# One load for the value rows of a block's neighbouring chunks, memory rows copied by GpSimd, and a planner that counts eight transfers: a fused attention and two-layer MoE kernel on one core

## The chip, the core and the metric

The kernel runs on one core of a Trainium2 chip. The metric is the device time of the whole program in microseconds (us). The core has TensorE for matrix products, VectorE, ScalarE and GpSimd for elementwise work, SyncE (SP) for issuing transfers, and 16 DMA engines that serve all queues. The profile calls the first four PE, DVE, ACT and POOL, PE's weight loads PEld, and SP's queue of transfers SPq.

## The reference: what is computed

```python
# attention, per batch and head: chunks of 32 queries, 16 keys to the left, 8 to the right, 8 memory keys
for c in range(nc):                       # B, H, S, D = 4, 8, 768, 64
    k_full = concat(mem_k, k[c*32-16 : c*32+40]);  v_full = concat(mem_v, v[same rows])
    scores = (q_c @ k_full.T) / sqrt(D)
    a = exp(scores - max); a = a / (sum(a) + 1e-9)
    out[c] = a @ v_full
x = out as 3072 tokens x 512
h = x @ w_in;  g = h * clip(h + 3, 0, 6) / 6;  x = g @ w_out          # layer 0, d_ff = 2048
h = x @ w_in2; g = where(h >= 1, h, where(h <= -1, 0, (h + 1)**2 / 4)); out = g @ w_out2   # layer 1
```

## The kernel before, in words

The 3072 tokens are worked in six tiles of 512 (`T`), and a tile is four attention blocks of 128 queries, that is four chunks of 32 (`NSB`). There are 24 blocks, numbered 0 to 23 here. The inputs lie in memory by groups of 96 queries (`QB`, index j). A group has a row block of queries and keys, and 120 rows of values: 8 memory rows, 16 to the left, 96, 8 to the right. For the first `NEARLY` groups queries, keys and values lie in one array `qkv` with value rows of 2 KB; for the later groups they lie in `qk` and `vv`, and a value row there comes in two pieces of 1 KB.

A block takes these steps. `load_block` brings queries and keys of a group (tile `q_sb`, 448 KB). `load_values` brings the values of the block's four chunks (tile `v_sb`, 512 KB: for each chunk 8 memory rows and 56 others). `scores` (L460) multiplies on PE into PSUM tiles `sc`; DVE and ACT make the softmax; DVE turns it (tile `tr`); `values` multiplies it on PE with `v_sb` into `pv` (L529 in blocks 0 to 7, L519 later); ACT and DVE write the result as a high and a low part (`xhi`, `xlo`). When four blocks are done, their tile goes through `hidden` (PE writes `ph`, L603 to L605: three products for each piece, high times high, high times low, low times high) and `project` (PE writes `py` in layer 0 and `po` in layer 1). The weights come packed (`raw`, 512 KB each, 64 of them) and are unpacked by ACT and DVE (L286 to L312) into `w`, two for each f of 16 in a layer.

The order of all work is made by a planner, `Plan`, before the program runs. Each task has a key (when it is due), the engines it can run on with an assumed duration, and the tiles it reads and writes; `run` steps through time and gives each engine its next task. The order on each engine is thus fixed at build time, and on the chip each engine takes its instructions in that order and waits where a tile is not ready. SP's order is the order in which it can issue loads. A load can't be issued before its tile's slot is free: the pool `in` has two slots (queries and keys), `lv` two (values), `o` two (outputs), `w` 33 (raw and unpacked weights, and for the first four blocks also loads and softmax tiles).

Up to a planned time of 60 us (`FILL`) the program puts unused products of a tile of zeros, here called fillers (L765), into gaps that the plan foresees on PE:

```python
while at + ns <= t.start + more:
    P.matmul(c, warm, warm[:, :n].unsqueeze(1).to_broadcast([128, m, n]), start=True, stop=True, ...)
    at += ns
```

Their number is part of the program and doesn't depend on what happens on the chip. In the trace each float32 product of `scores` and `values` (L460, L519, L529) is two matmuls, each with a weight load of its own, so `x128` in the trace is `x64` in a list of the program's order. All other products are one.

Of the kernel before, what the change touches and what calls it, by code (L numbers as in the profile page):

```python
# [10 lines left out]
F32 = mybir.dt.float32  # L11
# [22 lines left out]
GRP = 4  # L34
NEARLY = 6
LATE_W = GRP * (QB + KB)
# [36 lines left out]
WINDOW = 100  # L73
CHANGE = 100


class Plan:
# [58 lines left out]
    def run(self, at):  # L136
        free = dict(at)
        bw = 0
        last_kind = None
        ready = {e: [] for e in free}  # L140
# [10 lines left out]
        while left:  # L151
            best = None
            for e, ts in ready.items():
                found = []
                blocked = set()
                for t in sorted(ts, key=lambda t: (t.key, t.n)) if e == "SP" else ts:
                    est = max(free[e], t.ready)
                    taken = [] if blocked & {p for b in t.bufs if not b.slot for p in b.pools} else self.slots_for(t)
                    if taken is None or len(taken) < sum(b.slot is None for b in t.bufs):
                        if e == "SP":  # L160

                            blocked.update(p for b in t.bufs if b.slot is None for p in b.pools)
# [12 lines left out]
                if best is None or est < best[0]:  # L175
                    best = est, e, t
# [50 lines left out]
def fused_kernel(ctx: ExitStack, tc: tile.TileContext, qkv, qk, vv, wpk, const, out):  # L227
# [40 lines left out]
    def weight(l, f, z, key, after=()):  # L268
# [45 lines left out]
        lo, hi = (raw, "lo"), (raw, "hi")  # L314
        add(("SP", 430), key - 4, load, writes=[lo, hi], kb=512, after=after)
        add([("DVE", dve(512, True)), ("ACT", 575)], key - 0.5, shift, writes=[lo])
# [14 lines left out]

    q_buf, v_buf = {}, {}
    WQ = NP * (QB + KB)
# [9 lines left out]
    def load_block(j, key):  # L343
# [17 lines left out]
        if not wide(j):  # L361
            add(("SP", 430), key - 6 - far, lambda e: nc.sync.dma_start(tile_of(q), src), writes=[(q, 0)], kb=448, after=after, line="load")
            return
        k4 = lambda: tile_of(q)[:, NP * QB:].rearrange("p (a t) -> p a t", a=NP)
        add(
            ("SP", 430), key - 6 - far, lambda e: nc.sync.dma_start(
                k4()[:, :, :KB], src[:, NP * QB:].rearrange("p (a t) -> p a t", a=NP)
            ), writes=[(q, 1)], kb=256, after=after, line="load",
        )
        add(  # L370
            ("SP", 430), key - 6 - far, lambda e: nc.sync.dma_start(tile_of(q)[:, :NP * QB], src[:, :NP * QB]),
            writes=[(q, 0)], kb=192, after=after, line="load",
# [12 lines left out]
    def load_values(s, key):  # L385
# [5 lines left out]
            ["lv"] + ["w"] * early, [128, 2, H * D], F32, "v_sb", **({"w": 1} if early else {}),  # L391
        )
        runs = []
        for c in range(NSB):
            j, i = divmod(s * NSB + c, NCH)
            cuts = [0] + [NMEM] * (i > 0) + [CHUNK] * (not late) + [KC]
            for a, b in zip(cuts, cuts[1:]):
                row = a if b <= NMEM else a + CHUNK * i
                p, col = (64 * (c % 2) + a, c // 2) if late else (CHUNK * c + a % CHUNK, a // CHUNK)
                for r in runs:  # L400
# [5 lines left out]
        for n, (j, row, p, col, m) in enumerate(sorted(runs, key=lambda r: (r[3], r[2]))):  # L406
            if j < NEARLY:
                src, rows = qkv[j, row:row + m, WQ:], lambda t: t
            else:
                g = 2 * (j - NEARLY)  # L410
                src, rows = vv[g:g + 2, row:row + m, :].rearrange("g k c -> k g c"), lambda t: t.rearrange("k (g c) -> k g c", g=2)
            add(
                ("SP", 430), key - 5 - 3 * (not early),
                lambda e, src=src, rows=rows, p=p, m=m, col=col: nc.sync.dma_start(rows(tile_of(v)[p:p + m, col]), src),
                writes=[(v, n)], kb=2 * m, line="load v",
            )
        v.parts = len(runs)

    def block(s, key):
# [90 lines left out]
        def values(e, m=None):  # L510
# [25 lines left out]
        add(  # L536
            ("PE", 750 if all(wide(j) for j in qs) else 1450), key - 4, scores,
            [(q_buf[j], x) for j in qs for x in range(1 + wide(j))],
# [10 lines left out]
        add(("DVE", dve(512)), key - 2.4, norm, [(sm, 3)], [(st, 0), (st, 1)])  # L549
        of_v = [(v, n) for n in range(v.parts)]  # L550
        if late:
            for c in chunks:
                for b in range(2):
                    add(("DVE", dve(256)), key - 2.2, lambda e, c=c, b=b: turn_part(e, c, b), [(st, 0), (st, 1)], [(tr, c, b)])
            ts = [(tr, c, b) for c in chunks for b in range(2)]
            add(("PE", 750), key - 1, values, [*ts, *of_v], [(x, 0) for x in pv], line="values", kind="a")
        else:
# [130 lines left out]
    def second_x(n):  # L688
        xhi, xlo = xbuf[NT + n]
        key = NK + NF * n  # L690
        for c in range(NC):
            x = Buf(["in", "o", "st"], [128, T], F32, "x2raw")
            add(
                ("SP", 430), key - 8 + 0.5 * c, lambda e, c=c, x=x: nc.sync.dma_start(tile_of(x), ymid[n, :, c]),
                [("ymid", n, c)], [(x, 0)], kb=256, after=[h_tasks[key - NF]],
# [140 lines left out]
```

## Time and profile before

| | |
|---|---|
| time before, median of 3 runs | 1162.21 us (1161.91 to 1163.37) |
| time of the profiled execution | 1161.94 us |
| its span in the trace | 1160.1 us |
| PE busy in the span | 1144.1 us, 99% |
| DVE, ACT, POOL busy | 614.9, 457.8, 0.2 us |
| first product of `hidden` starts | 54.42 us |

The trace counts from the start of the span; 1.8 us of the execution's time lie outside it. PE is busy nearly throughout, but the fillers count as busy too, so the busy share says little of the first 55 us.

### The profile page before, as it was taken

The page shows a single profiled execution, that of the slowest core. Times are in us where ns is not written, and L with a number is a line of the kernel's source. Part 1 is how long each engine was busy: PE and PEld are TensorE (multiplying, and loading weights), DVE is VectorE, ACT ScalarE, POOL GpSimd, SP SyncE. Part 2 cuts the span into 40 slices and gives each one's busy share as a digit, 9 for nine tenths or more (in the row PEclk, how much of TensorE's full clock was granted, in tenths as well). Part 3 has the DMA queues.
Part 4 walks back from the last instruction along what each step waited for, and adds up shares of the span by engine and source line. Part 5 has one row for each costly group of instructions (what it writes and reads, how often), then busy time and mean ns, then how long its engine had stood idle before and what let it go on. Part 6 is the DMA issues. An engine that isn't in the chain of part 4 may idle for free.

```text
span 1160.1 us, 20860 instructions
## 1 busy us (share of the span) xinstructions
PE 1144.1 (99%) x8766; PEld 939.5 (81%) x8766; DVE 614.9 (53%) x1116; ACT 457.8 (39%) x1083; POOL 0.2 (0%) x4
## 2 busy tenths in 40 slices
PE   8899999999999999999999999999999999999998
PEld 6687888888887888888888888888888888888887
DVE  2589955445555445643899634434434434433433
ACT  3599633334333333333788423223223223222221
POOL 0000000000000000000000000000000000000000
PEclk8699999999999999999999999999999999999999
DMA  6791131112112112210656300200200200000100
GB/s 207 249 396 55 57 100 35 51 54 90 48 35 87 51 51 74 70 38 19 200 183 216 91 1 1 73 1 1 73 1 1 73 1 1 37 1 1 37 1 37
DMA packets 48644, 81.05 MB, mean 70 GB/s; under 512 B 5158, under 2 KB 28582, under 8 KB 48550
## 3 DMA queue, kind: packets, MB, share of 16 engines
q1 hardware_dynamic: 48550, 79.71, 20.9%
q8 instruction: 69, 1.13, 0.4%
q14 instruction: 25, 0.20, 0.1%
HBM read 67.11 MB, written 12.58 MB: 69 GB/s over the span
## 4 chain that ended last, share of the span: by engine, by line
PE 97%; DMA 1%; issue 1%; ACT 1%; DVE 0%; SPq 0%; DVEq 0%; ACTq 0%
PE ph L603 15%; PE ph L604 15%; PE ph L605 15%; PE py L652 8%; PE po L657 8%; PE po L659 8%; PE po L658 8%; PE py L653 7%; PE py L654 7%; PE sc L460 2%; PE pv L529 2%; PE pv L519 1%; PE pv L765 1%; DMA ymid<-ysb 0%; DMA v_sb<-qkv 0%
## 5 line engine op out<-in xcount | busy, mean ns | idle before, releaser
L603 PE MATMUL ph<-xhi,w 128*128 128x512 f32 x768 | 300.5, 391 | 0.0
L604 PE MATMUL ph<-xlo,w 128*128 128x512 f32 x768 | 299.2, 390 | 0.0
L605 PE MATMUL ph<-xhi,w 128*128 128x512 f32 x768 | 299.0, 389 | 0.0
L626 ACT ACTIVATE r<-r,bias 128x512 f32<-128x512 f32 x96 | 69.3, 722 | 286.6 <-DVE r L623 286.6
L633 DVE TENSOR_TENSOR glo<-r,ghi 128x512 fp32r<-128x512 f32 x192 | 132.6, 690 | 81.9 <-ACT ghi L632 80.4
L632 ACT CAST ghi<-r 128x512 fp32r<-128x512 f32 x192 | 119.5, 623 | 133.7 <-DVE r L629 71.2
L603 PEld LDWEIGHTS ph<-xhi,w 128*128 128x128 f32 x768 | 144.5, 188 | 30.5 <-ACT raw L286 0.3
L605 PEld LDWEIGHTS ph<-xhi,w 128*128 128x128 f32 x768 | 144.3, 188 | 30.2
L604 PEld LDWEIGHTS ph<-xlo,w 128*128 128x128 f32 x768 | 144.5, 188 | 29.7
L652 PE MATMUL py<-ghi,w 128*128 128x512 f32 x384 | 153.5, 400 | 1.3 <-DVE ysb L679 1.3
L654 PE MATMUL py<-ghi,w 128*128 128x512 f32 x384 | 149.8, 390 | 0.0
L653 PE MATMUL py<-glo,w 128*128 128x512 f32 x384 | 149.8, 390 | 0.0
L657 PE MATMUL po<-w,ghi 128*128 128x512 f32 x384 | 149.4, 389 | 0.0
L658 PE MATMUL po<-w,ghi 128*128 128x512 f32 x384 | 149.4, 389 | 0.0
L659 PE MATMUL po<-w,glo 128*128 128x512 f32 x384 | 149.4, 389 | 0.0
L619 DVE SCALAR_TENSOR_TENSOR r<-r,ph 128x512 f32<-128x512 f32 x96 | 65.8, 685 | 154.0 <-ACT r L616 153.3
L623 DVE TENSOR_SCALAR r<-ph 128x512 f32<-128x512 f32 x96 | 66.3, 691 | 152.2 <-PE ph L605 152.2
L616 ACT ACTIVATE r<-ph,bias 128x512 f32<-128x512 f32 x96 | 66.2, 689 | 191.9 <-PE ph L605 191.9
L629 DVE TENSOR_TENSOR r<-ph,r 128x512 f32<-128x512 f32 x96 | 66.3, 690 | 74.7 <-ACT r L626 74.7
L652 PEld LDWEIGHTS py<-ghi,w 128*128 128x128 f32 x384 | 72.0, 188 | 18.4 <-DVE ysb L679 1.7
L654 PEld LDWEIGHTS py<-ghi,w 128*128 128x128 f32 x384 | 72.1, 188 | 15.2
L659 PEld LDWEIGHTS po<-w,glo 128*128 128x128 f32 x384 | 72.1, 188 | 15.0
(52 smaller groups left out, 962.7 us busy)
## 6 DMA issues: line engine op xcount, KB each, us to landing
raw<-wpk SPq DMA_DIRECT2D x64, 512.0 KB
ymid<-ysb SPq DMA_DIRECT2D x24, 256.0 KB
x2raw<-ymid SPq DMA_DIRECT2D x24, 256.0 KB
out<-osb SPq DMA_DIRECT2D x24, 256.0 KB
q_sb<-qk SPq DMA_DIRECT2D x21, 256.0 KB
v_sb<-vv SPq DMA_DIRECT2D x43, 112.0 KB
q_sb<-qk SPq DMA_DIRECT2D x21, 192.0 KB
v_sb<-vv SPq DMA_DIRECT2D x24, 128.0 KB
```

What stands on the lines that cost most here:

```text
L603: P.matmul(p, whi[:, c, :], xh[:, c, :], start=(c == 0), stop=False)
L604: P.matmul(p, whi[:, c, :], xl[:, c, :], start=False, stop=False)
L605: P.matmul(p, wlo[:, c, :], xh[:, c, :], start=False, stop=(c == NC - 1))
L626: add(("ACT", act(T) + 100), k + 0.35, lambda e: A.activation(out=rt(), in_=rt(), func=AF.Square, bias=bias[:, 1:2], scale=0.5,), [], [(r, ...
L632: add(("ACT", act(T)), k + 0.5, lambda e: A.copy(tile_of(ghi), rt()), [(r, 0)], [(ghi, 0)])
L633: add(("DVE", dve(T)), k + 0.6, lambda e: V.tensor_tensor(out=tile_of(glo), in0=rt(), in1=tile_of(ghi), op=ALU.subtract,), [(r, 0), (ghi, ...
L652: P.matmul(y, w2hi, gh, start=first, stop=False)
L653: P.matmul(y, w2hi, gl, start=False, stop=False)
L654: P.matmul(y, w2lo, gh, start=False, stop=last)
L657: P.matmul(y, gh[:, t], wt[:, 0], start=first, stop=False)
L658: P.matmul(y, gh[:, t], wt[:, 1], start=False, stop=False)
L659: P.matmul(y, gl[:, t], wt[:, 0], start=False, stop=last)
```

## The change

Four things are edited. `NEARLY` goes from 6 to 11, so that all groups of blocks 0 to 7 lie in `qkv`. For these blocks `load_values` no longer loads memory rows and other rows apart. One transfer takes all chunks of the block that lie in one group: to each partition two value rows, the chunk's row r and row r + 32 of the group. What lands on the partitions of the memory rows is then wrong for a chunk that isn't the first of its group, and GpSimd copies the right 8 rows there from a tile `vm`, which POOL's own queue loads once per batch. The planner's `run` holds back an SP transfer until the eighth transfer before it has ended (`LANES`). And some assumed durations change. The weights, the products and the arithmetic stay.

```diff
-NEARLY = 6
+NEARLY = 11
+LANES = 8
@@ def run(self, at):
+                    if e == "SP" and len(lanes) >= LANES:
+                        est = max(est, lanes[-LANES])
...
-                t.end = bw
+                lanes += [bw] * (e == "SP")
+                t.end = bw if e == "SP" else t.end + 1900 + t.kb / 0.1
@@ durations: loads of SP 430 -> 450, late v loads 430 -> 800; scores 750 -> 800; late values 750 -> 1070, turn_part 337 -> 450
@@ def load_values(s, key):
+        if not late:
+            v.parts = []
+            at = s * SB // S
+            if at not in m_buf:
+                vm = m_buf[at] = Buf(["o"], [128, H * D], F32, "vm")
+                for c in range(NSB):
+                    add(("POOL", 600), key - 6, lambda e, p=CHUNK * c: nc.gpsimd.dma_start(
+                        tile_of(vm)[p:p + NMEM], qkv[at * NQB, :NMEM, WQ:]), writes=[(vm, c)], kb=16)
...
+                rows = qkv[j, CHUNK * i:CHUNK * (i + n), WQ:]
+                src = bass.AP(rows.tensor, rows.offset, [rows.ap[0], [CHUNK * rows.ap[0][0], 2], rows.ap[1]])
...
+                add(("SP", 470), key - 5, lambda e, src=src, p=CHUNK * c, n=n: nc.sync.dma_start(
+                    tile_of(v)[p:p + CHUNK * n], src), writes=[part], kb=180 * n, line="load v")
+                for x in range(c + (i == 0), c + n):
+                    v.parts.append((v, "m", x))
+                    add(("POOL", 900), key - 4.5, lambda e, j=j, p=CHUNK * x: G.tensor_copy(
+                        tile_of(v)[p:p + NMEM, 0], tile_of(vm)[p:p + NMEM]), [part, (vm, x)], [(v, "m", x)])
...
-            cuts = [0] + [NMEM] * (i > 0) + [CHUNK] * (not late) + [KC]
+            cuts = [0] + [NMEM] * (i > 0) + [KC]
```

Since the planner decides the order, the order on the engines changes too. On SP the program begins, before the change, with two groups and then the values of block 0 in eight transfers:

```order
L362 DMA q_sb<-qkv 128x896 x2
L414 DMA v_sb<-qkv 32x512
L414 DMA v_sb<-qkv 8x512
L414 DMA v_sb<-qkv 24x512
L414 DMA v_sb<-qkv 8x512
L414 DMA v_sb<-qkv 24x512
L414 DMA v_sb<-qkv 32x512
L414 DMA v_sb<-qkv 96x512
L414 DMA v_sb<-qkv 32x512
L362 DMA q_sb<-qkv 128x896
```

After the change SP begins with these rows:

```order
L369 DMA q_sb<-qkv 128x896 x2
L423 DMA v_sb<-qkv 96x2x512
L423 DMA v_sb<-qkv 32x2x512
L369 DMA q_sb<-qkv 128x896
L423 DMA v_sb<-qkv 64x2x512 x2
L369 DMA q_sb<-qkv 128x896
L423 DMA v_sb<-qkv 32x2x512
L423 DMA v_sb<-qkv 96x2x512
L369 DMA q_sb<-qkv 128x896 x2
```

The eight values transfers of a block have become two of the same bytes, so that the fourth group of queries and keys (`q_sb`) is the 8th transfer and no longer the 21st. Further down SP's queue, before the change, 16 weights stand ahead of the groups 8 and 9:

```order
L414 DMA v_sb<-vv 96x2x256
L279 DMA raw<-wpk 128x512 x16
L362 DMA q_sb<-qk 128x896 x2
L279 DMA raw<-wpk 128x512 x6
```

After the change the values of blocks 4 and 5 and the groups 8 and 9 stand ahead of these 16 weights, and 16 other weights are already issued:

```order
L423 DMA v_sb<-qkv 64x2x512 x2
L286 DMA raw<-wpk 128x512 x6
L423 DMA v_sb<-qkv 32x2x512
L423 DMA v_sb<-qkv 96x2x512
L369 DMA q_sb<-qkv 128x896 x2
L286 DMA raw<-wpk 128x512 x16
```

The groups 8 and 9 go into the two slots of `in`, which are free when `scores` of block 5 has read the groups 6 and 7. On PE the first `values` stood, before the change, right behind 50 fillers, and `scores` of block 2 behind it:

```order
L765 LDWEIGHTS warm
L765 MATMUL pv<-warm 128x128
L529 MATMUL pv<-tr,v_sb 64x32 x64
L460 MATMUL sc<-q_sb 32x8 x6
L460 MATMUL sc<-q_sb 32x56 x2
```

After the change `scores` of block 2 stands ahead of the first `values`, and fillers behind it:

```order
L503 MATMUL sc<-q_sb 32x56 x2
L503 MATMUL sc<-q_sb 32x64 x2
L503 MATMUL sc<-q_sb 32x56 x4
L572 MATMUL pv<-tr,v_sb 64x32 x64
L808 LDWEIGHTS warm
L808 MATMUL pv<-warm 128x128
```

In all, PE's order up to the first product of `hidden`, with matmuls counted as the trace counts them, is this. Before: 26 fillers, scores 0 (96), 15 fillers, scores 1 (112), 50 fillers, values 0 (128), scores 2 (112), 11 fillers, values 1 (128), 6 fillers, scores 3 (96), 42 fillers, values 2 (128), 5 fillers, scores 4 (112), 42 fillers, values 3 (128), 8 fillers of 512 columns: 1245 matmuls. After: 26 fillers, scores 0, 15 fillers, scores 1, 15 fillers, scores 2, values 0, 23 fillers, values 1, scores 3, 55 fillers, values 2, scores 4, 18 fillers, values 3, 8 fillers of 512 columns: 1200 matmuls. Behind that, before: 12 products of `hidden`, 17 fillers, scores 5. After: 24 products of `hidden`, 2 fillers, scores 5, and further on 8 fillers of 512 columns. From about the second half of the first tile on, the two orders on PE are the same.

## Rows read from the trace of the kernel before

**Rows 1.** The page, parts 1 and 3: busy time by engine; a DMA queue's packets, MB, share

```profile
PE 1144.1 (99%) x8766; PEld 939.5 (81%) x8766; DVE 614.9 (53%) x1116; ACT 457.8 (39%) x1083; POOL 0.2 (0%) x4
...
q8 instruction: 69, 1.13, 0.4%
```

**Rows 2.** The chain that ended last, 0 to 62 us: start us, us, what

```profile
5.95 3.91 DMA q_sb<-qkv
...
10.86 0.33 issue
...
17.23 1.90 issue
...
23.08 1.58 issue
...
29.10 1.41 issue
...
39.05 0.50 issue
...
44.57 2.95 issue
...
51.86 0.38 issue
```

**Rows 3.** Timeline of PE: start us, us, line, output<-input, count, idle before

```profile
30.51 0.96 PE L460 MATMUL sc<-q_sb 64*32 64x64 f32 x49 [1.41 <-issue]
31.39 4.66 PE L765 MATMUL pv<-warm 128*128 128x128 bf16 x42
35.98 2.10 PE L529 MATMUL pv<-tr,v_sb 32*64 32x32 f32 x128
...
47.52 3.37 PE L529 MATMUL pv<-tr,v_sb 32*64 32x32 f32 x125 [2.95 <-issue]
...
52.24 2.74 PE L765 MATMUL ph<-warm 128*128 128x512 bf16 x6 [0.38 <-issue]
54.42 0.99 PE L603 MATMUL ph<-xhi,w 128*128 128x512 f32 x1
...
58.39 2.03 PE L765 MATMUL sc<-warm 128*128 128x256 bf16 x17
```

**Rows 4.** Packets of the DMA queues, 0 to 54.4 us: packets, MB, share

```profile
q8 instruction: 10, 0.16, 1.2%
```

**Rows 5.** Windows: stretch, length, PE, PEld, DVE, ACT, POOL busy, granted clock, DMA share, GB/s

```profile
11.19:19.13 7.94, 6.04 (x255) 5.63 (x254) 4.91 (x14) 3.55 (x21) 0.00 (x0) 0.99 0.49 144
19.13:24.66 5.53, 3.95 (x127) 3.48 (x126) 0.93 (x3) 0.00 (x0) 0.00 (x0) 0.50 0.91 275
24.66:30.51 5.85, 4.44 (x129) 3.47 (x129) 0.97 (x4) 4.45 (x22) 0.00 (x0) 0.50 0.86 292
30.51:39.55 9.04, 8.54 (x254) 7.80 (x255) 5.54 (x15) 3.24 (x21) 0.00 (x0) 0.69 0.66 215
39.55:47.52 7.97, 5.02 (x127) 4.67 (x128) 3.98 (x8) 2.86 (x7) 0.00 (x0) 0.71 0.99 360
47.52:52.24 4.72, 4.34 (x128) 3.28 (x127) 2.10 (x7) 2.33 (x7) 0.00 (x0) 0.50 0.41 124
54.40:136.00 81.60, 81.51 (x1072) 65.76 (x1071) 76.44 (x147) 72.52 (x188) 0.00 (x0) 0.99 0.50 186
```

**Rows 6.** Timeline of SP's queue, first microseconds

```profile
1.65 4.13 SPq L414 DMA_DIRECT2D v_sb<-qkv  x8
5.95 0.35 SPq L362 DMA_DIRECT2D q_sb<-qkv  x1
```

**Rows 7.** Timelines of POOL and ACT: its first memset, and a copy of 512 columns

```profile
0.24 0.10 POOL L826 MEMSET const-float32-0.0<- 128x1 f32 x1 [0.24 <-issue]
...
39.52 0.68 ACT L261 CAST w<-raw 128x512 fp32r<-128x512 f32 x1
```

**Rows 8.** Windows, as Rows 5, of the stretch in which blocks 6 and 7 load

```profile
90.00:120.00 30.00, 30.00 (x358) 24.38 (x351) 28.62 (x54) 29.18 (x69) 0.00 (x0) 1.00 0.15 43
```

More of the change, by code (lines that the diff above doesn't have):

```diff
@@ L138, in run @@
         bw = 0
+        lanes = []
         last_kind = None
@@ L314, in weight @@
         lo, hi = (raw, "lo"), (raw, "hi")
-        add(("SP", 430), key - 4, load, writes=[lo, hi], kb=512, after=after)
+        add(("SP", 450), key - 4, load, writes=[lo, hi], kb=512, after=after)
         add([("DVE", dve(512, True)), ("ACT", 575)], key - 0.5, shift, writes=[lo])
@@ L361, in load_block @@
         if not wide(j):
-            add(("SP", 430), key - 6 - far, lambda e: nc.sync.dma_start(tile_of(q), src), writes=[(q, 0)], kb=448, after=after, line="load")
+            add(("SP", 450), key - 6 - far, lambda e: nc.sync.dma_start(tile_of(q), src), writes=[(q, 0)], kb=448, after=after, line="load")
             return
@@ L392, in load_values @@
         )
+        if not late:
[4 more added lines that the diff above has]
+                for c in range(NSB):
+                    add(
+                        ("POOL", 600), key - 6, lambda e, p=CHUNK * c: nc.gpsimd.dma_start(
+                            tile_of(vm)[p:p + NMEM], qkv[at * NQB, :NMEM, WQ:]
+                        ), writes=[(vm, c)], kb=16,
+                    )
+            vm = m_buf[at]
+            c = 0
+            while c < NSB:
+                j, i = divmod(s * NSB + c, NCH)
+                n = min(NSB - c, NCH - i)
+                rows = qkv[j, CHUNK * i:CHUNK * (i + n), WQ:]
+                src = bass.AP(rows.tensor, rows.offset, [rows.ap[0], [CHUNK * rows.ap[0][0], 2], rows.ap[1]])
+                part = (v, c)
+                v.parts.append(part)
+                add(
+                    ("SP", 470), key - 5, lambda e, src=src, p=CHUNK * c, n=n: nc.sync.dma_start(
+                        tile_of(v)[p:p + CHUNK * n], src
+                    ), writes=[part], kb=180 * n, line="load v",
+                )
+                for x in range(c + (i == 0), c + n):
+                    v.parts.append((v, "m", x))
+                    add(
+                        ("POOL", 900), key - 4.5, lambda e, j=j, p=CHUNK * x: G.tensor_copy(
+                            tile_of(v)[p:p + NMEM, 0], tile_of(vm)[p:p + NMEM]
+                        ), [part, (vm, x)], [(v, "m", x)],
+                    )
+                c += n
+            return
         runs = []
@@ L416, in load_values @@
             )
-        v.parts = len(runs)
+        v.parts = [(v, n) for n in range(len(runs))]
     def block(s, key):
@@ L536, in block @@
         add(
-            ("PE", 750 if all(wide(j) for j in qs) else 1450), key - 4, scores,
+            ("PE", 800 if all(wide(j) for j in qs) else 1450), key - 4, scores,
             [(q_buf[j], x) for j in qs for x in range(1 + wide(j))],
@@ L549, in block @@
         add(("DVE", dve(512)), key - 2.4, norm, [(sm, 3)], [(st, 0), (st, 1)])
-        of_v = [(v, n) for n in range(v.parts)]
+        of_v = v.parts
         if late:
@@ L553, in block @@
                 for b in range(2):
-                    add(("DVE", dve(256)), key - 2.2, lambda e, c=c, b=b: turn_part(e, c, b), [(st, 0), (st, 1)], [(tr, c, b)])
+                    add(("DVE", 450), key - 2.2, lambda e, c=c, b=b: turn_part(e, c, b), [(st, 0), (st, 1)], [(tr, c, b)])
             ts = [(tr, c, b) for c in chunks for b in range(2)]
-            add(("PE", 750), key - 1, values, [*ts, *of_v], [(x, 0) for x in pv], line="values", kind="a")
+            add(("PE", 1070), key - 1, values, [*ts, *of_v], [(x, 0) for x in pv], line="values", kind="a")
         else:
```

12 lines of the change are left out of this document (6 added, 6 removed).

## Prediction, before the changed kernel had run

> **What bounds the kernel now.** I read the page first: PE is busy 99% of the span [rows 1], so only time in which PE does no useful product can be won. The windows say where it is. From 54.40 to 136.00 us PE is busy 81.51 of 81.60 us [rows 5]; behind that its order is the same in both programs, so whatever moves the start of `hidden`, at 54.42 us [rows 3], moves the end by as much. The start-up is the place.
>
> What fills the 54 us? The chain of waits shows PE's own work broken by pieces called "issue": 0.33, 1.90, 1.58, 1.41, 0.50, 2.95 and 0.38 us, 9.05 us together [rows 2]. In these PE waits for no tile. The windows cut at the ends of these pieces show the pattern: from 19.13 to 24.66 us PE starts 127 matmuls, from 39.55 to 47.52 again 127, from 24.66 to 30.51 and from 47.52 to 52.24 a count that differs from it by the matmuls at the edge, and from 11.19 to 19.13 and 30.51 to 39.55 twice as many [rows 5]. A pause of this kind comes only after each 127th matmul, in the midst of equal ones: 3 products of `values`, a pause, then the other 125 [rows 3]. The queue q8 explains the number: 1.13 MB over 2 x 8766 instructions of PE is 64 bytes for one, and 0.16 MB in 10 packets is 16 KB each, or 256 instructions [rows 1, 4], that is 127 matmuls with weight loads and two others. So PE's instructions come by DMA, in packets of 127 matmuls, and PE waits at a packet's end when the next one isn't there.
>
> How long a packet takes goes with the loads beside it. Per packet: 3.97 us at 144 GB/s, 4.72 at 124, 4.52 at 215, 5.53 at 275, 5.85 at 292, 7.97 at 360 [rows 5] (the first and third are halves of a window with two). PE is busy 5.02 of the last 7.97 us, and some of that is fillers: 42 in 4.66 us in the stretch before [rows 3].
>
> The Trainium skill (Runtime: NRT & Kernel Launch, "Instruction fetch mechanics") says that instructions come in 16 KiB blocks, the next being fetched while the current one runs, and that crossing a block's border is mostly hidden. The size agrees with rows 4; "hidden" does not, here. By the page the pauses would be nothing, which is the third rival below.
>
> **The change, part by part.**
>
> *Loads of blocks 0 to 7.* The 8 or 9 value transfers of a block become 2 with the same bytes. Before, SP issued 8 of them in 4.13 us, and the third group of queries and keys could go out only at 5.95 us [rows 6], landing 3.91 us later [rows 2], at 9.86, where scores 1 waited for it. That load is now the fifth and the wait goes, but PE only comes sooner to the pause of 10.86 us [rows 2], whose end depends on the instruction packet: I take 0. Behind it no load stands in the chain before `hidden`, so earlier data alone wins nothing more. What the change does to the loads is to make them dense: with eight transfers in flight of 128 to 512 KB, in place of many of 16 and 64 KB, the 15.2 MB ahead of groups 8 and 9 (8 groups of 448 KB, 6 blocks of 512, 16 weights of 512) run without gaps. At the 360 GB/s of rows 5 they take 42 us. Before, the windows from 11.19 to 39.55 us add up to 6.3 MB, 223 GB/s on average. So five instruction packets now come under load that came under 144 to 292 before.
>
> *The price of a packet under load* is the term that decides. Bounds: 4.34 us, the mean of the three light rows (7.94 + 4.72 + 9.04 over 5 packets), if load didn't matter; 7.97, the row nearest in GB/s. I take 6.1, a little above the rows at 275 and 292, since the loads in flight are largely smaller than in the 7.97 row, where weights were loaded, and since SP must pause at the values of block 4 until `values` 0 is done.
>
> *PE's new order.* Packet ends lie at matmul 223 and every 127 after: 350, 477, 604, 731, 858, 985, 1112, 1239. Before, `hidden` starts behind matmul 1245, and waits for all nine; now behind 1200, and waits for eight. The walk:
> - 223 (in scores 1): before 11.19; under load the packet is 6.1 - 4.34 = 1.8 later: 13.0.
> - 350, 477, 604, 731 (scores 2, values 0, values 1, scores 3): 4 x 6.1 = 24.4: 37.4, where before it was 30.51.
> - 858: 20 matmuls of scores (0.96/49 each, 0.4), 55 fillers (4.66/42 each, 6.1), 52 of values (2.10/128 each, 0.85) [rows 3] are 7.3, over 6.1, so no pause: 44.7.
> - 985 and 1112: the loads have run out at some 42 us, as groups 8 and 9 wait for scores 5. Two light packets, 8.7: 53.4.
> - 80 of values at 3.37/125 (2.2) and 8 fillers at 2.74/6 (3.65) [rows 3]: `hidden` at 59.2.
>
> Against 54.42 that is 4.8 us later. Granted clock: half, 1.2 GHz, in most of these windows [rows 5]; I keep the durations of those rows.
>
> *Behind it.* Packet 1239 now ends behind 24 products of `hidden`, 5 us of work that hide it. Fillers: before 17 in 2.03 us [rows 3], now 2 of the same and 8 of 512 columns at 0.228 (the step between two products of `hidden`, 1.81 us for eight): 2.06. DVE's order has 8 unpacking steps ahead of the last `xlo` of the first tile, as before, so its 76.44 of 81.60 us [rows 5] shift with PE. The 16 last weights go out behind scores 5, at some 66 us; 16 have landed by then, enough for half the tile. I take 0.
>
> *GpSimd.* 8 transfers and 21 copies on an engine that did nothing; no row has their price. A transfer costs an issuing queue about 0.5 us (4.13/8, rows 6); a copy lies between POOL's memset of one column, 0.10, and ACT's copy of 512 columns, 0.68 [rows 7]. At the upper end block 0's copies are done at 0.7 + 4.1 + 1.4 = 6.2 us or when its load lands; `values` 0 starts at about 19. That cover, 13 us, hides copies and transfers several times as dear; if it were gone, each further us would delay `values` 0. The copies of blocks 6 and 7 fall into a stretch where DVE is busy 28.62 of 30 us [rows 8]; if a copy held DVE up for its whole length, 5 x 0.68 - 1.38 = 2.0 us would be lost. I take 0, as 16 of the 21 lie where DVE waits; 0 to 2.0 goes into the range. The Trainium skill (SBUF — State Buffer, "SBUF: two separate sides") has the rule behind this: GpSimd and VectorE share a port pair that one instruction holds to its end. No run shows it yet.
>
> *The rest.* New durations for late blocks change the plan; on PE nothing moves there: 0. The tile `vm` adds 8 x 16 KB of loads on POOL's queue, 0.3 us at 360 GB/s, beside the others: 0.
>
> Sum: 1161.94 (the profiled execution, span 1160.1 and 1.8 around it) + 4.8 = 1166.7; the median of the runs is 0.27 above that execution, so **1167.0**.
>
> **The rivals.**
> 1. *Slower by the packets* (forecast): a loaded packet at 5.6 to 8. At 5.6 the five give 2.3 us, at 7.97 14.1: 1164.5 to 1176.4. For: the six rows rise with GB/s. Against: 215 and 292 differ by little, and only one row is near 360.
> 2. *No change*: a loaded packet at 5.14 +/- 0.46, that is the average before (41.05 us over eight), gives 1162.2 +/- 2.3. For: rows at 275; the lost packet (45 matmuls fewer) then pays for the fuller queue.
> 3. *Faster*: a packet's wait has a ceiling that doesn't grow with what is in flight. At 4.34 all packets are light: -4.0, 1158.2. Below 5.15 it decides for faster. The Trainium skill (DMA: Bandwidth & Descriptors, "Queues, rings and completion order") speaks for it: each engine turns between queues by packets, so an instruction packet should wait for one packet of loads, not all. No row here shows that ceiling. If pauses vanished altogether: 54.42 - 9.05 = 45.4, 1153.2.
> 4. *GpSimd late*: its copies gate `values`. It decides once 8 transfers and 2 copies take over 18 us, four times the upper rows; 3 us more on top of rival 1, 1170. Against: that cover.
>
> **How the numbers follow.** Less than 0.2%, 2.3 us, can't be told from no change. Chances: rival 1 0.50, rival 2 0.20, rival 3 0.26 (0.05 of it without pauses), rival 4 0.04. So slower 0.54, same 0.20, faster 0.26. Range 1156 to 1175: below lie the vanished pauses, above packets at the 7.97 bound throughout or with GpSimd late; about 2 in 10 left out. The likeliest case alone has 1164 to 1176.
>
> **What would show it.** Right: pauses called "issue" at the named matmuls; GB/s over 330 from 13 to 37 us; 5.6 to 7 us between pauses there; `hidden` between 56 and 61 us; no PE wait on POOL; the rest of the span, 1105.7 us, unchanged. Wrong: packets of 4 to 5 us under full load, or `hidden` before 52 us (then rival 3); PE waiting on POOL or on a load; a PE wait between 60 and 136 us, which would mean that DVE was the bound.

## The result, and the profile after

The changed kernel takes 1172.19 us, the median of four runs (1167.6 to 1172.74). The kernel before took 1162.79 beside it on the same chip (four runs, 1161.91 to 1165.07). The ratio is 1.0069, 95% interval 1.004 to 1.0099: slower, by 9.4 us in the medians. The prediction was 1167.0 with 1156 to 1175, and 0.54 on slower.

The profiled execution took 1167.6 us, the shortest of the four; the other three took 1172.05 to 1172.74. So the trace below accounts for 5.7 of the 9.4 us (span 1165.8, before 1160.1); the 3.7 left are in no trace.

The page of the changed kernel, parts 1 and 3, answers to [rows 1]:

```profile
PE 1140.3 (98%) x8714; PEld 935.8 (80%) x8714; DVE 616.3 (53%) x1110; ACT 462.4 (40%) x1089; POOL 19.4 (2%) x33
...
q8 instruction: 68, 1.11, 0.4%
```

The timeline of PE in the changed kernel, where before had [rows 3] (start, us, line, operation, count, idle before and its releaser):

```profile
10.18 0.96 PE L503 MATMUL sc<-q_sb 64*32 64x8 f32 x78 [1.52 <-DMA q_sb<-qkv]
14.80 0.53 PE L503 MATMUL sc<-q_sb 64*32 64x8 f32 x26 [3.66 <-issue]
22.09 0.52 PE L503 MATMUL sc<-q_sb 64*32 64x8 f32 x25 [2.12 <-issue]
28.54 1.06 PE L572 MATMUL pv<-tr,v_sb 32*64 32x32 f32 x26 [3.35 <-issue]
34.72 1.70 PE L572 MATMUL pv<-tr,v_sb 32*64 32x32 f32 x51 [0.67 <-issue]
43.31 0.51 PE L503 MATMUL sc<-q_sb 64*32 64x8 f32 x20 [5.72 <-issue]
53.06 0.81 PE L503 MATMUL sc<-q_sb 64*32 64x64 f32 x62 [1.28 <-issue]
56.72 1.43 PE L572 MATMUL pv<-tr,v_sb 32*64 32x32 f32 x80 [0.91 <-issue]
60.72 0.99 PE L646 MATMUL ph<-xhi,w 128*128 128x512 f32 x1
```

These are the only long idle times between the first product and `hidden`. Seven are called "issue", 17.7 us against 9.05 before [rows 2], and they stand where the prediction had put them: ahead of matmuls 223, 350, 477, 604, 731, 985 and 1112, and none at 858 (within one matmul, by the trace's records). `hidden` starts at 60.72, 6.3 us later than before; the rest of the span is 1105.1 us, before 1105.7. So all of what the trace shows was lost in the start-up.

Windows of the changed kernel, cut at those ends, answer to [rows 5] (stretch, length, busy of PE, PEld, DVE, ACT, POOL, granted clock, DMA share, GB/s):

```profile
14.80:22.09 7.29, 5.17 (x128) 3.63 (x128) 2.69 (x6) 2.68 (x17) 1.82 (x3) 0.50 1.06 284
22.09:28.54 6.45, 3.10 (x128) 2.82 (x127) 2.61 (x7) 0.43 (x2) 1.56 (x2) 0.50 1.02 391
28.54:34.72 6.18, 5.51 (x126) 5.12 (x127) 1.36 (x6) 1.11 (x7) 0.00 (x0) 0.50 1.02 406
34.72:43.31 8.59, 2.87 (x127) 2.63 (x128) 0.61 (x3) 3.14 (x18) 1.30 (x3) 0.50 1.05 278
43.31:53.06 9.75, 8.47 (x253) 8.01 (x253) 6.83 (x19) 5.50 (x25) 1.13 (x2) 0.74 0.81 263
53.06:56.72 3.66, 2.75 (x128) 2.45 (x127) 2.60 (x4) 1.30 (x3) 2.04 (x2) 1.00 0.02 4
60.70:136.00 75.30, 74.08 (x976) 59.03 (x975) 72.25 (x137) 69.08 (x179) 4.10 (x5) 0.99 0.44 157
```

In the first six rows one packet of 127 matmuls goes to a row (two in the fifth). DMA share is the mean busy share of the 16 DMA engines. While the DMA engines are full (share over 1) a packet takes 6.18 to 8.59 us, 7.13 on average; when the loads have run out it takes 3.66. The sixth and the fourth row have nearly the same busy time of PE, 2.75 and 2.87 us, and differ by 4.9 us. The last row is new in kind: PE is idle for 1.2 us behind the start of `hidden`, where before it was idle for 0.09 [rows 5].

The traces also show when a packet's bytes are moved. With the view of the DMA queues cut into windows of 0.1 us, one 16 KB transfer of q8 stands ahead of the end of each pause. Some of them (us; the last two columns are differences):

| trace, and the load beside the packet | PE resumes | transfer starts | PE resumes again | resuming to start | start to resuming |
|---|---|---|---|---|---|
| before, loaded | 39.55 | 45.1 | 47.52 | 5.6 | 2.4 |
| changed, loaded | 14.80 | 19.2 | 22.09 | 4.4 | 2.9 |
| changed, loaded | 34.72 | 40.5 | 43.31 | 5.8 | 2.8 |
| changed, loads run out | 53.06 | 54.2 | 56.72 | 1.1 | 2.5 |
| e8 (below), no load | 21.16 | 22.4 | 24.89 | 1.2 | 2.5 |
| e8, weights | 83.94 | 87.7 | 90.14 | 3.8 | 2.4 |

Over the pauses of before, the changed kernel, e5, e7, e8, e9 and e12, PE resumes 2.2 to 3.2 us after the start of a transfer, with load or without. What load lengthens is the time until the transfer starts. So PE waits for these 16 KB: this is seen in the traces and not only inferred from the count of matmuls.

### The profile page after: what moved, and what is told of

The parts are those of the page before. It is cut to its first block, busy times and chain, and to the rows that moved or that the text cites. A ratio compares the mean times of both kernels' runs of the same rounds, so it can differ in the third digit from the quotient of the medians.

```text
span 1165.8 us, 20769 instructions
## 1 busy us (share of the span) xinstructions
PE 1140.3 (98%) x8714; PEld 935.8 (80%) x8714; DVE 616.3 (53%) x1110; ACT 462.4 (40%) x1089; POOL 19.4 (2%) x33
## 4 chain that ended last, share of the span: by engine, by line
PE 96%; issue 2%; DVE 1%; DMA 1%; ACT 0%; SPq 0%; DVEq 0%; ACTq 0%
PE ph L646 15%; PE ph L647 15%; PE ph L648 15%; PE py L695 8%; PE po L700 7%; PE po L702 7%; PE po L701 7%; PE py L696 7%; PE py L697 7%; PE sc L503 2%; PE pv L572 2%; PE pv L562 1%; PE pv L808 1%; DMA q_sb<-qkv 1%; PE ph L808 0%
## 5 line engine op out<-in xcount | busy, mean ns | idle before, releaser
L676 DVE TENSOR_TENSOR glo<-r,ghi 128x512 fp32r<-128x512 f32 x192 | 132.6, 691 | 87.7 <-ACT ghi L675 86.6
L700 PEld LDWEIGHTS po<-w,ghi 128*128 128x128 f32 x384 | 72.1, 188 | 15.0
```

The source lines that it names most:

```text
L676: add(("DVE", dve(T)), k + 0.6, lambda e: V.tensor_tensor(out=tile_of(glo), in0=rt(), in1=tile_of(ghi), op=ALU.subtract,), [(r, 0), (ghi, ...
L700: P.matmul(y, gh[:, t], wt[:, 0], start=first, stop=False)
```

## The experiments

Each but e8 and e12 was compared with the kernel before on its own chip (1160.1 to 1162.2 us in the medians). "Hidden" is the start of `hidden` in the profiled execution, "rest" is the span behind it.

| run | us, median | ratio, 95% interval | hidden | rest |
|---|---|---|---|---|
| before | 1162.79 | | 54.42 | 1105.7 |
| changed kernel | 1172.19 | 1.0069 [1.004, 1.0099] | 60.72 | 1105.1 |
| e1, changed, no fillers | 1167.2 | 1.0054 [1.0035, 1.0074] | 57.74 | 1107.7 |
| e2, before, no fillers | 1153.46 | 0.9939 [0.9922, 0.9955] | 47.12 | 1104.1 |
| e3, changed, fillers in halves | 1175.44 | 1.0131 [1.0112, 1.015] | 65.75 | 1107.1 |
| e4, before, 24 extra transfers | 1191.04 | 1.0262 [1.0244, 1.028] | 82.05 | 1107.6 |
| e5, changed, weights late | 1175.58 | 1.0143 [1.0115, 1.017] | 64.42 | 1108.3 |
| e6, before, planner's rule alone | 1164.69 | 1.0038 [1.0025, 1.0051] | 54.48 | 1110.1 |
| e7, before, 12 extra stores | 1165.8 | 1.0048 [1.0033, 1.0063] | 58.40 | 1107.1 |
| e9, changed, no planner's rule | 1177.88 | 1.0142 [1.0115, 1.0169] | 69.10 | 1106.1 |
| e10, changed, copies twice | 1172.76 | 1.0094 [1.0063, 1.0126] | 63.64 | 1111.0 |
| e11, planner's rule, no fillers | 1157.36 | 0.9956 [0.9938, 0.9974] | 46.90 | 1107.8 |

### Is it the number of instructions? e1, e2, e3

e1 (of the changed kernel) and e2 (of the kernel before):

```diff
-FILL = 60000
+FILL = 0
```

e3, of the changed kernel, gives two fillers of half the width for each:

```diff
 _, m, n = c.shape
+c, n = c[:, :, :n // 2], n // 2
```

> The changed kernel without its fillers (170 products of a tile of zeros that nothing reads); all else as in the changed kernel. Theory (the start-up is set by instruction packets of PE, 127 matmuls each, at some 7 us each under load): 1040 matmuls in place of 1200 stand ahead of hidden, so one packet fewer, and the 8 wide fillers ahead of hidden (3.2 us) go: hidden at 50 to 53 us in place of 60.7, time 8 to 10 us below the changed kernel. Rival (the softmax chain and the loads set the start-up; fillers only fill time that is lost anyway): hidden within 3.5 us of 60.7. Second rival (fillers keep TensorE's granted clock up): products behind 60 us at 1.2 GHz and a longer time.

> The kernel before without its fillers. Theory: 1040 matmuls in place of 1245 ahead of hidden, two packets fewer at about 5 us: hidden at 44 to 47 us in place of 54.4, time about 1153 to 1155. Rival (fillers only fill time that is lost anyway): hidden at 51 to 54.

> The changed kernel with each filler cut into two of half the columns, so nearly twice as many instructions for the same columns. Theory: some 160 matmuls more ahead of hidden, 1.26 packets: hidden 5 to 9 us later than 60.7, at 66 to 70, time 5 to 9 us above the changed kernel. Rival (columns and clock count, not instructions): within 2 us of the changed kernel.

e2 and e3 came within 0.3 us of what the packets ask: without its fillers the kernel before starts `hidden` at 47.12; with its fillers cut in two, the same columns in more instructions, the changed kernel starts it at 65.75, behind 1362 matmuls in place of 1200. e1 missed: 57.74, not 50 to 53, and by the ratios it is some 2 us below the changed kernel, not 8 to 10. By its own condition, within 3.5 us of 60.7, the rival that fillers only fill time that is lost anyway came true there. Half of it holds: in e1 PE waits 15.5 us for tiles ahead of `hidden`, where in the changed kernel it waits 1.5, but 18.7 us of pauses called "issue" stay. Windows of e1:

```profile
0.00:20.00 20.00, 6.09 (x351) 5.29 (x351) 5.32 (x18) 6.65 (x35) 9.98 (x20) 1.00 0.95 249
20.00:40.00 20.00, 7.86 (x323) 7.26 (x324) 6.14 (x19) 6.92 (x41) 1.22 (x2) 1.00 1.03 349
40.00:60.00 20.00, 11.90 (x373) 10.74 (x374) 9.30 (x23) 8.34 (x23) 3.66 (x6) 1.00 0.56 177
```

The loads fill the DMA engines well beyond 40 us whatever PE does (share 0.95, 1.03, 0.56). Between 20 and 40 us 323 matmuls start, 7.9 us to each 127, some of it in waits for tiles; in the changed kernel 380 start there, fillers included. So most of the 160 matmuls fewer are saved behind that stretch, where packets are cheaper. The rival that fillers hold the clock up fell: the granted clock is 1.00 in all three rows without them, and 0.50 in the first four windows of the changed kernel with them.

### Is it the load beside the packets? e4, e5, e7

e4 sends 24 transfers of 512 KB from memory to memory on GpSimd's queue at the start. e7, milder, sends 12 stores of 512 KB from SBUF once block 1's values have landed:

```diff
+    junk = dram.tile([12, 128, 2, H * D], F32, name="junk")
...
+            if t is v_buf[1].last:
+                for i in range(12):
+                    G.dma_start(junk[i], tile_of(v_buf[1]))
```

e5, of the changed kernel, plans all weights but the first behind the load of block 4's values:

```diff
-    for s in range(m):
+    for s in range(m + 1):
         loads(s)
+    gate = [plan.last["load v"]]
...
-        weight(0, f, 0, f - 3)
-        weight(0, f, 1, f - 1)
+        weight(0, f, 0, f - 3, gate if f > 1 else ())
+        weight(0, f, 1, f - 1, gate if f > 0 else ())
...
-        if s >= m:
+        if s > m:
```

> The kernel before, with 24 transfers of 512 KB from memory to memory on POOL's queue at the start, which nothing reads: PE's and SP's order and all waits as before, only more load on the DMA engines (12.6 MB read and written). Theory: packets that took 4 to 5.5 us take 6 to 8 while these transfers run; hidden at 60 to 70 us, with pieces called issue longer at the same matmuls. Rival (the new order of PE or GpSimd made the changed kernel slower, not the load): pieces called issue as before, 9 us together, and hidden at 54 to 56, unless loads of tiles become late, which the chain would show as DMA.

> The kernel before, with twelve stores of 512 KB from SBUF to an unused array in memory, on GpSimd's queue, which go out once block 1's values have landed, at some 12 us. No other instruction moves; only bytes are added beside the packets. The first loads are not disturbed, as they have landed by then. Theory (packets by load): from 13 to about 40 us the traffic is over 320 GB/s, the packets that end in it take 6 to 8 us (5.5 and 5.9 before), hidden starts at 58 to 64 us, with the growth in the pieces called issue; total 1164 to 1172. Rival (load does not matter for a packet): packets as before, hidden at 54 to 56, total within 2.5 us of before. If a load of scores or values waits instead, the chain will show DMA there, and that part of the growth is no packet's.

> The changed kernel, but all weights except the first three are planned behind the load of block 4's values, which itself waits for the first values product. So the queue is nearly idle while the packets that end at matmuls 477 and 604 are fetched, and the same bytes of weights go out afterwards. Theory (a packet costs by the load that runs beside it): the packets that end where the load has paused take 4 to 5.2 us (6.45 and 6.18 in the changed kernel), those beside the thirteen weights take 6.5 to 8.5 and the light tail of the changed kernel (9.75 us for two) goes; hidden starts between 57 and 61 us, the total 1164 to 1169. Rival (a packet costs the same wherever it lies, and the count of packets or the new order of PE sets the start): the packets behind 350 take 6 to 7 us each with no dip, hidden at 60 to 62. Rival (the weights are late and PE waits for them): a wait for raw or its parts at the start of hidden, which then begins after 62 us.

e4 says nothing of packets: the extra transfers held up the first loads themselves. This one piece of its chain is longer than the delay of `hidden`, 27.6 us:

```profile
12.28 29.05 DMA v_sb<-qkv
```

e7 is the clean form. PE's order is that of before to the last instruction. Its windows, for the packets that end at matmuls 604 and 731:

```profile
20.46:27.62 7.16, 3.95 (x127) 3.47 (x126) 0.93 (x3) 0.00 (x0) 1.59 (x3) 0.50 1.02 369
27.62:34.29 6.67, 4.43 (x128) 3.47 (x128) 0.98 (x4) 3.25 (x20) 0.00 (x0) 0.50 1.03 412
```

Before, these two took 5.53 and 5.85 us [rows 5], with PE busy 3.95 and 4.44 us: the same busy time to 0.01. What rose is the load, from 275 and 292 GB/s with a share of 0.91 and 0.86, and with it the packets, by 1.63 and 0.82 us. `hidden` moved by 4.0 us to the lower edge of what was expected; 0.67 of it is a wait for ACT's softmax, which the chain leads back to a late load of weights. So load alone, with no instruction moved, makes packets longer.

e5 missed its times (`hidden` at 57 to 61, total 1164 to 1169), and bore out one of the two light packets that I expected. The timeline of PE and four windows of e5:

```profile
29.55 1.05 PE L572 MATMUL pv<-tr,v_sb 32*64 32x32 f32 x26 [3.47 <-issue]
30.54 2.63 PE L809 MATMUL pv<-warm 128*128 128x128 bf16 x23
33.10 2.32 PE L572 MATMUL pv<-tr,v_sb 32*64 32x32 f32 x128
...
40.53 0.51 PE L503 MATMUL sc<-q_sb 64*32 64x8 f32 x20 [4.28 <-issue]
```

```profile
23.14:29.55 6.41, 2.94 (x127) 2.72 (x126) 2.53 (x7) 0.43 (x2) 0.90 (x2) 0.53 0.73 285
29.55:33.17 3.62, 3.62 (x53) 3.36 (x55) 0.99 (x4) 0.45 (x2) 0.00 (x0) 0.50 0.30 79
40.53:52.97 12.44, 8.06 (x253) 7.49 (x253) 8.72 (x21) 5.79 (x25) 0.00 (x0) 0.77 1.03 389
52.97:60.52 7.55, 4.50 (x129) 4.02 (x128) 0.00 (x0) 0.00 (x0) 1.82 (x3) 0.50 1.02 301
```

Where the queue was idle (79 GB/s), matmul 604 falls in the midst of the 128 values at 33.10 with no pause. But the packet that ends at 477 took 6.41 us, as in the changed kernel (6.45), though the loads ran out in its midst, at some 27 us: its transfer started only then, at 27.0, 3.8 us after PE had resumed. So a gap helps a packet only if it is there when the transfer is to start. The weights that were held back then lie beside the packets up to 1112, which in the changed kernel had less beside them: 12.44 us for two and 7.55, against 9.75 and 3.66. Bytes put off within the start-up come back on later packets.

### A packet by itself: e8, e12

In both all of the computation is left out. PE runs 39 stretches of 127 equal small products; SP loads beside them. e8:

```diff
+        run(acc[0], 12)
+        run(acc[1], 1)
...
+        for i in range(48):
+            nc.sync.dma_start(small[i % 8][:8], ...)
+        for i in range(60):
+            nc.sync.dma_start(raw[i % 8], wpk[i // 32, i % 32 // 2, i % 2])
+        run(acc[2], 26)
```

e12 has three kinds of load in place of these: `wide` (queries and keys, 30 x 448 KB), `vals` (values in the changed kernel's form, 34 x 384 KB), and `raw` (26 x 512 KB).

> All of the computation is left out; the output holds only marks. PE runs equal small products back to back, in stretches of 127 matmuls that need nothing but their instructions: first with no load in flight, then beside 48 loads of 16 KB, then beside 60 loads of 512 KB one after the other. A product here takes less than 0.03 us when its instructions are there, so a packet's 127 take under 4 us and the interval between pauses is the packet's own time. Theory: intervals of 3 to 4.5 us without load, 6.5 to 8 us beside the dense loads. Rival (a packet's time has a ceiling that load does not move): the same interval in both stretches, within 0.5 us. Rival (instructions are fetched ahead and never waited for): no pauses of over 0.2 us at every 127th matmul.

> All of the computation is left out; the output holds only marks. PE runs equal small products in stretches of 127 matmuls, first with nothing beside them, then beside 30 loads of queries and keys (448 KB), then 34 loads of values in the changed kernel's form (384 KB in pieces of 2 KB), then 26 of weights (512 KB). Beside dense weights a packet took 6.2 us when measured alone, and 7.1 on average in the changed kernel. Theory A (the form of the loads sets the difference): the packets beside the loads of values take 7 us or more, those beside weights 6.2. Theory B (a packet costs 6.2 us beside any dense load, and what is over it in the changed kernel comes from the products themselves and the tiles they wait for): 5.9 to 6.5 in all three stretches.

The timeline of PE in e8, two rows without load and two with, and windows of the stretches without and with weights:

```profile
21.16 3.35 PE L243 MATMUL acc<-warm 128*128 128x32 bf16 x128 [0.38 <-issue]
24.89 3.35 PE L243 MATMUL acc<-warm 128*128 128x32 bf16 x128 [0.38 <-issue]
...
83.94 3.58 PE L243 MATMUL acc<-warm 128*128 128x32 bf16 x128 [2.72 <-issue]
90.14 3.52 PE L243 MATMUL acc<-warm 128*128 128x32 bf16 x128 [2.62 <-issue]
```

```profile
10.53:61.62 51.09, 46.64 (x1787) 45.52 (x1784) 0.68 (x2) 0.00 (x0) 1.00 0.08 23
84.00:139.80 55.80, 31.89 (x1152) 31.14 (x1152) 0.00 (x0) 0.00 (x0) 0.65 1.03 407
```

A packet takes 3.73 us without load and beside the loads of 16 KB, of which 3.35 are its products, and 6.2 beside weights at 407 GB/s, with the same products. The pause at its end grows from 0.38 to 2.6 us. Both rivals fall; the 6.2 is a little below the 6.5 that I expected. Windows of e12, for six, seven and six packets beside the three kinds:

```profile
53.46:85.15 31.69, 21.00 (x769) 20.51 (x768) 0.00 (x0) 0.00 (x0) 0.68 0.95 334
92.17:133.07 40.90, 24.70 (x896) 24.12 (x896) 0.00 (x0) 0.00 (x0) 0.71 1.06 264
139.54:172.88 33.34, 21.07 (x769) 20.57 (x769) 0.00 (x0) 0.00 (x0) 0.69 0.98 354
```

That is 5.3, 5.8 and 5.6 us a packet. Both theories of e12 fall in their strict form: the values do not stand out on the mean (single ones took 7.0, just ahead of this window, and 6.7, others 4.8), and the range is 4.6 to 7.0 rather than 5.9 to 6.5. What it shows is that GB/s is the wrong scale: beside values at 264 GB/s a packet costs no less than beside weights at 354. The DMA share, near 1 in all three, is what they have in common.

### The parts of the change: e6, e9, e10, e11

e6 is the kernel before with the planner's rule alone, and e11 that with `FILL = 0`:

```diff
+LANES = 8
...
+                    if e == "SP" and len(lanes) >= LANES:
+                        est = max(est, lanes[-LANES])
...
-                t.end = bw
+                lanes += [bw] * (e == "SP")
+                t.end = bw if e == "SP" else t.end + 1900 + t.kb / 0.1
```

e9 is the changed kernel with `LANES = 100000`: new loads and copies, without the rule. e10 is the changed kernel with each `G.tensor_copy` issued twice.

> The kernel before, with the planner's rule of eight transfers in flight alone; the many small transfers of values stay. The first 37 transfers keep their order and sizes, so up to 30 us the loads beside the packets are those of before; hidden moves from behind matmul 1245 to behind 1226, that is ahead of the packet end at 1239, and has nineteen fillers fewer ahead of it or behind. Theory (packets by load): packets up to 731 as before within 0.6 us each, hidden at 52 to 55 us, total within 2.5 us of before (0.998 to 1.002). Rival (the planner's order of PE, not the loads, made the changed kernel slower): hidden at 58 us or later, total at least 4 us above before.

> The changed kernel, but with its planner told that any number of transfers may be in flight, so that the loads by tiles and GpSimd's copies are tried without the planner's rule. PE's order up to hidden stays nearly that of the changed kernel (1200 matmuls ahead), and fifteen loads of weights stand in one row ahead of block 4's values, so the queue is dense until some 40 us. Theory (dense loads beside the packets make the start late): packets of 6 to 8 us from 13 to 40 us, hidden at 58 to 62 us, total 1164 to 1171. Rival (the planner's rule carries most of the change's cost): hidden as in the changed kernel or earlier, total within 2.5 us of before.

> The kernel before with the planner's rule of eight transfers alone, and without any fillers. Theory (with the rule alone it was the nineteen fillers behind the first products of hidden, and the wait at the packet end there, that cost 4 us, not the order of loads): hidden at 46 to 48 us as in the kernel before without fillers, total 1152 to 1156. Rival (the rule's order of the late loads and of PE costs it): hidden at 46 to 48 but the rest of the span 3 us or more longer than the 1104.1 us there, total 1156.5 to 1160.

> The changed kernel with each of GpSimd's 21 copies of memory rows done twice; PE's, DVE's and SP's orders stay. Theory (GpSimd lies under the cover of the packets and of the loads): same as the changed kernel within 2.5 us, no PE wait on POOL, hidden at 59 to 62 us. Rival (the copies hold DVE up by the port that they share, or gate the values): 21 x 0.6 to 0.97 us more of GpSimd, of which the five or so where DVE is busy throughout would cost 3 to 5 us, total 1175 or more, or a PE wait on POOL.

e9 shows that the planner's rule doesn't carry the loss: without it the loss is larger. What is left of the change is the loads by tiles, with the copies, the new durations and the order that comes of them. The durations, and PE's new order with the old loads, were not run by themselves. The timeline of PE in e9:

```profile
41.09 0.50 PE L503 MATMUL sc<-q_sb 64*32 64x8 f32 x20 [3.25 <-issue]
49.58 1.42 PE L572 MATMUL pv<-tr,v_sb 32*64 32x32 f32 x76 [2.21 <-issue]
57.87 1.02 PE L503 MATMUL sc<-q_sb 64*32 64x64 f32 x62 [6.25 <-issue]
64.04 2.23 PE L572 MATMUL pv<-tr,v_sb 32*64 32x32 f32 x80 [1.68 <-issue]
```

With all weights in one row the queue stays full, and from 15.32 to 57.87 us six packets take 7.09 us each, and the seventh 6.17. That is the changed kernel's price, 7.13, paid for three packets more; `hidden` comes at 69.10 and the total is 1177.88, both beyond what I had expected (58 to 62, and 1164 to 1171). The planner's rule therefore gave back 8.4 us of start-up in the changed kernel.

On the kernel before, the rule alone did nothing to the start-up (54.48, as expected) and lost 4.4 us behind it, which neither theory of e6 had; the total is 4.1 us above before, where I had expected at most 2.5. e11 put that loss to the test, and my theory (the fillers behind `hidden`) fell: without any fillers the rest is still 3.7 us longer than in e2, and 1157.36 lies where the rival, the rule's new order, had it. Its chain from 52 us on shows why:

```profile
52.01 0.69 ACT r L622
52.70 0.57 ACT raw L292
53.39 1.30 ACT st L491 x8
54.74 0.77 PE ph L609
```

Behind 12 products of `hidden` PE stands for 2.8 us until ACT has done a softmax, queued behind `r` and a weight's unpacking. e6 has the same wait of 2.75 us in its trace. It is the rule's new order on ACT, not a packet.

e10's ratio can't be told from the changed kernel's: 1.0094 and 1.0069, with intervals that overlap. Its `hidden`, 63.64, came 1.6 us beyond what was expected, with PE never waiting on POOL. But its trace does not bear out a price of nothing for GpSimd. Timelines of e10, POOL, DVE and PE:

```profile
113.80 5.79 POOL L430 COPY v_sb<-vm 8x512 f32<-8x512 f32 x6 [10.20 <-DMA v_sb<-qkv]
...
117.00 1.09 DVE L676 TENSOR_TENSOR glo<-r,ghi 128x512 fp32r<-128x512 f32 x1
119.04 0.59 DVE L534 TENSOR_SCALAR sm<-sm 128x8 f32<-128x8 f32 x1
...
122.07 2.10 PE L572 MATMUL pv<-tr,v_sb 32*64 32x32 f32 x64 [2.42 <-ACT raw L299]
```

The same place in the changed kernel, where three copies run from 110.12 to 112.77 us:

```profile
110.12 1.62 POOL L430 COPY v_sb<-vm 8x512 f32<-8x512 f32 x2 [11.17 <-DMA v_sb<-qkv]
...
104.03 1.28 DVE L303 SCALAR_TENSOR_TENSOR raw<-raw 128x512 uint32<-128x512 uint32 x2
...
111.20 2.11 DVE L303 SCALAR_TENSOR_TENSOR raw<-raw 128x512 uint32<-128x512 uint32 x2
113.23 0.68 DVE L676 TENSOR_TENSOR glo<-r,ghi 128x512 fp32r<-128x512 f32 x1
114.44 0.16 DVE L534 TENSOR_SCALAR sm<-sm 128x8 f32<-128x8 f32 x1
...
117.04 1.53 PE L572 MATMUL pv<-tr,v_sb 32*64 32x32 f32 x64 [1.21 <-DVE tr L547]
```

A DVE step that meets copies is longer: the same pair takes 2.11 in place of 1.28 us, and with the copies doubled three more steps grow, the two shown, 0.68 to 1.09 and 0.16 to 0.59, and the one between them, 0.68 to 1.09. Behind it PE waits 1.21 us in the changed kernel and 2.42 in e10: 1.21 more, where the three steps grew by 1.25 together. In e10's profiled execution, its longest of four (1176.38), the granted clock is half from 122.6 to 129.5 us after that wait, and the products of `hidden` there stand 0.43 us apart in place of 0.23. The rule of the Trainium skill that stands in the prediction (SBUF — State Buffer, "SBUF: two separate sides"), one instruction holding the port pair to its end, agrees with these longer steps; the runs don't tell it from other contention.

## Why the prediction was right

**The mechanism** held. The pauses stood at the named matmuls, each ends 2.4 to 2.9 us after the start of an instruction transfer, e7 reproduced them by load alone, e3 by the number of instructions, and e8 by themselves. Right side, right place; the median lies 5.2 us above the number, and two terms were mis-sized. That the traced 5.7 us came so near to the forecast 4.8 is in part luck, since the errors of these two terms nearly cancel.

Of the signs that the prediction named, 344 GB/s from 13 to 37 us, `hidden` at 60.72, no wait on POOL and the unchanged rest came true. Two packets took longer than the 5.6 to 7 us named, 7.29 and 8.59. And two of its signs of being wrong showed, both small: PE waited 1.52 us for a load, and 1.21 us for DVE at 117 us.

**The price of a packet under load** was taken as 6.1 us, and measured 7.13 over the four from 14.80 to 43.31, 4.1 us in all. That is inside the bounds, nearer to the upper one. Alone, beside one kind of load, a packet costs 5.3 to 6.2 (e8, e12); beside mixed loads 7.1 in the changed kernel and in e9. Why the mixture costs 1 us more stays open. The packets of 8.59 us, and of 8.49 and 8.29 in e9, are those whose transfer started latest, 5.7 to 5.8 us after PE had resumed; for the other three dense ones in the changed kernel it was 3.7 to 4.4. Why so late stays open too. Both reasons for a middle value failed. Smaller loads did not make cheaper packets: 5.8 us beside values of 384 KB, 5.6 beside weights of 512 KB (e12). And the pause of SP at the values of block 4, 28.5 to 29.7 us, left no gap: the DMA share is 1.02 in the row that holds it. The 8.59 came at 278 GB/s, so GB/s is not the scale. The DMA share, which stood in the same [rows 5], parts them better: under 5 us up to 0.66, over 5.5 from 0.86.

**The first packet** resumed at 14.80, not 13.0. The wait of scores 1 for its load, which I had let go, stayed (1.52 us): the group is fifth in the queue and scores 1 still waited for it until 10.18, where before it was 9.90. In this it cost nothing, as the pause behind it ends with the packet.

**The light tail** was taken too dear, and hid most of this. From 43.31 to 60.72 are 17.4 us, forecast 37.4 to 59.2, 21.8: the three packets and the last products were shorter (9.75 us for the two up to 985, forecast 11.6; 3.66 for the packet from 985 to 1112, forecast 4.35; 4.00 from there to `hidden`, forecast 5.85). The prediction had kept the durations of rows at half clock; here the granted clock was 0.74 and 1.00 in the two windows shown and 0.73 in the last 4.00 us, which is part of it. So 5.9 us too little in the dense part, 4.4 too much behind it: 1.5 off at `hidden`.

**GpSimd at 0 to 2.0.** The copies took 0.60 to 1.14 us each, 0.71 on average, the transfers 0.53, and PE never waited on POOL: right for the start-up. Behind it a wait of 1.21 us came, of which the 0.83 that DVE lost beside copies is the visible part. The bound held, the 0 did not; since the rest of the span came out 0.6 us shorter all the same, it did not decide.

**Fillers and the rest at 0** held for the profiled execution. The 4.6 us by which the median of the changed kernel exceeds it are in no trace. Three things on record point at where they may lie. The granted clock over the whole span was 0.983 there and 0.979 to 0.981 in the other three runs; by an estimate from these clocks, 2 to 5 us if PE was the bound then. The first 26 fillers, the same in each of these programs, took 4.42 us there and 4.52 in e9, but 5.14 to 5.73 in before, e4, e5, e6, e7 and e10, so up to 1.3 us. And e10's wait and half clock, 5.9 us of rest, are of that size. But in e10's four runs the clock does not order the times (0.982 for 1176.38, 0.980 for 1171.78), and that any of this made those runs longer is only argued.

**The rivals.** No change needed packets of 4.68 to 5.6 us by its own band, and faster packets below that; the 5.15 that rival 3 names is only the price at which nothing changes. No dense packet in the changed kernel took less than 6.18. The ceiling of rival 3 (the Trainium skill, DMA: Bandwidth & Descriptors, "Queues, rings and completion order") does show in part: alone, a packet costs 5.3 to 6.2 on average, and in e8 its transfer starts some 2.5 us later beside weights than without load, less than the 5.4 to 6.0 us that a load takes from issue to landing in e12 (medians of its three kinds), so it does not seem to wait for all that is queued; but that ceiling lies above 5.15. What the Trainium skill calls "mostly hidden" (Runtime: NRT & Kernel Launch, "Instruction fetch mechanics") holds without load, 0.38 of 3.73 us, and fails with it, 2.6 of 6.2.

**Better than both kernels** is e2: the kernel before without its fillers, 0.9939 [0.9922, 0.9955]. They were instructions, and instructions were what PE waited for. The granted clock rose too, to 1.00 from 0 to 80 us, so e2 alone doesn't say how much of its gain is instructions; e3 does, at equal columns, with 5.0 us for 162 more of them.

## What to carry to other kernels

When an engine pauses with nothing to wait for, count its instructions between pauses; an equal count, and a transfer on the instruction queue ahead of each pause's end, mean that it waits for the instructions themselves, and then each instruction, each filler too, and each load that fills the DMA engines beside it has a price, unless the engine would wait for a tile there anyway, as in e1. Fewer and larger transfers can lose there: they left no gaps for the instructions here. Price such a stretch by the DMA share and by how long the loads last, not by GB/s; bytes that are only put off within it come back on later packets, so take instructions out first.

## What the runs showed that I had not expected

- Without fillers the granted clock was 1.00 from 0 to 80 us in e1, with PE busy only 6.09, 7.86 and 11.90 of each 20 us; with them it was 0.50 from 14.80 to 43.31 us. In e8 it was 1.00 in the unloaded stretches and 0.65 beside the loads, with PE busy 57%. A busier PE was not a faster one; what decides it, these runs do not tell.
- The price of a packet does not follow GB/s: 5.8 us at 264, 5.3 at 334, 6.2 at 407 (e12, e8).
- A GpSimd copy of 8 x 512 elements, 0.71 us on average, seems to lengthen even a DVE step of 8 columns from 0.16 to 0.59 us.
